# K and V loads of 8 MB in place of 4 MB, in an overlapping ring and a fixed buffer

## The chip, the cores and the metric

The kernel runs on one core of one Trainium2 chip. The metric is device time in microseconds (us), the median of several executions. Times of one kernel mostly repeat within about 0.1% here. The record calls a run slow when it is over 1.5% above the fastest of the same kernel.

## The reference, cut to what matters

One decoding step: attention of one query per head over a long cache of keys and values, times a small gated MLP.

```python
B, Sq, D = 2, 1, 512
Hq, Hkv, Sk, Dh = 32, 8, 32768, 128          # bf16 caches: B x Hkv x Sk x Dh
xn = layernorm(A_x)
q = (xn @ wq) ...                            # 4 query heads share one K/V head
p = softmax(q @ k^T * Dh ** -0.5)
s = (p @ v) ... @ wo
g = silu(mlp(xn))                            # w3, w4; w1 and w2 do not matter for one position
return A_x + s * g
```

K and V are 2 x 8 heads x 32768 x 128 x 2 bytes, 8 MB for each head and 268 MB in all. With the weights, 280.5 MB have to come from memory once, and each byte is used once. I call one (batch, K/V head) pair a head group; there are 16.

## The kernel before: the parts that matter

Each head group is cut into two halves of 16384 keys. A half of K, and a half of V, is one transfer of 4 MB: 128 partitions with 32 KB contiguous each. All large loads take the next of five equal slots.

```python
SLOT = KPT * Dh                              # 128 keys x 128: 32 KB per partition
slots = ctx.enter_context(tc.tile_pool(name="slots", bufs=5))

def load_cache(cache, b, g, i, name):
    t = slot(name)
    nc.sync.dma_start(
        out=t[:, :],
        in_=cache[b, g, i * NK:(i + 1) * NK, :].rearrange("(p t) d -> p (t d)", p=128),
    )
    return t
# ...
for n in range(NW + 1):                      # NW = 32 halves
    if n + 2 < NW:
        k_tiles[n + 2] = load_cache(A_k_cache, *work[n + 2], "k")
    if 0 < n + 1 < NW:
        v_tiles[n + 1] = load_cache(A_v_cache, *work[n + 1], "v")
    # ... at the last half: wo in three parts
    if n < NW:
        eps[n] = emit_k(n)                   # 8 transposes on DVE, 32 matmuls on PE, exp on ACT, pt on DVE
    if n == 1:
        emit_mlp()
    if n > 0:
        emit_v(n - 1, eps.pop(n - 1))        # 32 matmuls on PE
```

`emit_k` transposes a half of K on VectorE (eight operations into tile `T`) and multiplies it with the queries on TensorE. `emit_v` multiplies the exponentials `pt` with V.

The softmax here doesn't subtract the row's maximum and nothing guards it: scores larger than these inputs give would overflow.

Of the kernel before, what the change touches and what calls it, by code (L numbers as in the profile page):

```python
# [9 lines left out]
BF16 = mybir.dt.bfloat16  # L10
# [4 lines left out]
I32 = mybir.dt.int32  # L15

KPT = 128
RT = 16
VT = 4
SLOTS = 5  # L20
T_BUFS = 4
GELU_C = 0.7978845608028654
EPS = 1e-5
# [3 lines left out]
def kernel(  # L27
# [14 lines left out]
    nc = tc.nc  # L42

    B, Sq, D = A_x.shape
    _, Hkv, Sk, Dh = A_k_cache.shape
    HD = A_wq.shape[1]
    Hq = HD // Dh
# [2 lines left out]
    assert Sq == 1 and Dh == 128 and rep == 4 and D == 512 and Fdim % 128 == 0  # L50
    DK = D // 128
    FK = Fdim // 128
    NK = 128 * KPT
    assert Sk % NK == 0
    NPART = Sk // NK
    NR = KPT // RT
    NB = Dh // 64
    ZC = 128 + (NR - 1) * rep
# [2 lines left out]
    SLOT = KPT * Dh  # L61
# [2 lines left out]
    QP = 32 * (NQ - 1) + B  # L64

    pers = ctx.enter_context(tc.tile_pool(name="pers", bufs=1))
    slots = ctx.enter_context(tc.tile_pool(name="slots", bufs=SLOTS))
    ktp = ctx.enter_context(tc.tile_pool(name="ktp", bufs=T_BUFS))
    epp = ctx.enter_context(tc.tile_pool(name="epp", bufs=2))
    ptp = ctx.enter_context(tc.tile_pool(name="ptp", bufs=3))  # L70
# [4 lines left out]
    sc_ps = ctx.enter_context(tc.tile_pool(name="sc_ps", bufs=2, space=bass.MemoryType.PSUM))  # L75
    o_ps = ctx.enter_context(tc.tile_pool(name="o_ps", bufs=2, space=bass.MemoryType.PSUM))

    def slot(name):
        return slots.tile([128, SLOT], BF16, tag="slot", name=name)

    def load_cache(cache, b, g, i, name):
        t = slot(name)
        nc.sync.dma_start(
            out=t[:, :],
            in_=cache[b, g, i * NK:(i + 1) * NK, :].rearrange("(p t) d -> p (t d)", p=128),
        )
        return t


    x_bf = pers.tile([B, D], BF16)  # L90
    nc.scalar.dma_start(out=x_bf[:, :], in_=A_x[:, 0, :])
    wq_t = slot("wq")
    nc.sync.dma_start(  # L93
        out=wq_t[:, 0:DK * HD],
        in_=A_wq.rearrange("(p k) f -> p (k f)", k=DK),
# [3 lines left out]
    nc.gpsimd.memset(x4_bf[:, :], 0.0)  # L99
    for n in range(NQ):  # L100
        nc.gpsimd.dma_start(out=x4_bf[32 * n:32 * n + B, :], in_=A_x[:, 0, n * QW:(n + 1) * QW])
    work = [(b, g, i) for b in range(B) for g in range(Hkv) for i in range(NPART)]
    k_tiles, v_tiles = {}, {}
    k_tiles[0] = load_cache(A_k_cache, *work[0], "k0")
    k_tiles[1] = load_cache(A_k_cache, *work[1], "k1")
    w34 = slot("w34")
    W4O = DK * Fdim
    nc.sync.dma_start(out=w34[:, 0:W4O], in_=B_w3.rearrange("(p k) f -> p (k f)", k=DK))
    nc.sync.dma_start(out=w34[:, W4O:W4O + FK * D], in_=B_w4.rearrange("(p f) d -> p (f d)", f=FK))
    v_tiles[0] = load_cache(A_v_cache, *work[0], "v0")  # L110


    ident = pers.tile([128, 128], BF16)
# [6 lines left out]
    for j in range(4):  # L120
        nc.vector.tensor_copy(
            out=sel[:, :, :, j, :],
            in_=ident[:, :].rearrange("p (b w e) -> p b e w", b=NB, e=2),
# [4 lines left out]
        out=sel_o[:, :, :],  # L128
        in_=ident[:, :].rearrange("p (j a t h) -> p a t h j", j=4, t=VT, h=rep)[:, 0, :, :, :],
# [4 lines left out]
        out=sel_h[:, :],  # L134
        in_=ident[:, :].rearrange("p (r h) -> p h r", h=rep),
# [4 lines left out]
    for j in range(4):  # L140
        nc.vector.tensor_copy(
            out=sel_r[:, :, j, :],
            in_=ident[:, :].rearrange("p (w r) -> p r w", r=NQ),
# [3 lines left out]
    for r in range(NQ):  # L147
        nc.vector.tensor_reduce(
            out=mask[:, r, :],
            in_=ident[:, :].rearrange("p (h w) -> p h w", h=rep),  # L150
# [40 lines left out]
    for s, src in enumerate((xn_bf, ln2_bf)):  # L191
        for k in range(DK):
            c = (s * DK + k) * B
# [24 lines left out]
    for nb in range(NB):  # L218
# [9 lines left out]
        out=qr[:, :, :, :, :].rearrange("p n e b h -> p (n e b h)"),  # L228
# [54 lines left out]
            )  # L283
        return z

    def emit_k(n):
        b, g, i = work[n]
        if i == 0:
            state["z"] = emit_z(b, g)
        z = state["z"]  # L290
        kt = k_tiles.pop(n)[:, :].bitcast(I32)
        sc = sc_ps.tile([128, RT * 32], F32, tag="sc", name="sc")
        W = RT * NB * 32
        for r in range(NR):
            T = ktp.tile([128, W], I32, tag="T", name="T")
            nc.vector.transpose(  # L296
                out=T[:, :].rearrange("p (b t k) -> p t b k", b=NB, t=RT),
                in_=kt[:, r * W:(r + 1) * W].rearrange("p (t b k) -> p t b k", b=NB, t=RT),
            )
            Tb = T[:, :].bitcast(BF16).rearrange("p (b c e) -> p b c e", b=NB, e=2)  # L300
            zc = (NR - 1 - r) * rep
            for nb in range(NB):
                for e in range(2):
                    nc.tensor.matmul(  # L304
                        sc[:, :],
                        lhsT=z[:, nb, e, zc:zc + 128],
                        rhs=Tb[:, nb, :, e],
                        start=(r == 0 and nb == 0 and e == 0),
                        stop=(r == NR - 1 and nb == NB - 1 and e == 1),
                    )  # L310
        ep = epp.tile([128, RT * 32], BF16, tag="ep", name="ep")
        rs = smp.tile([128, 1], F32, tag="rs", name="rs")
        nc.scalar.activation(out=ep[:, :], in_=sc[:, :], func=ACT.Exp, scale=inv_sqrt_dh, accum_out=rs[:, :])  # L313
        pt = ptp.tile([128, NR, RT * rep], BF16, tag="pt", name="pt")
        nc.vector.transpose(  # L315
            out=pt[:, :, :].rearrange("p r (t h) -> p t r h", h=rep),
            in_=ep[:, :].rearrange("p (t r h) -> p t r h", r=NR, h=rep),
        )
        return pt, rs

    def emit_v(n, ep):
        b, g, i = work[n]
        pt, rs = ep
        vt = v_tiles.pop(n)[:, :].rearrange("p (t d) -> p t d", d=Dh)
        if i == 0:
            state["o"] = o_ps.tile([128, VT * Dh], F32, tag="o", name="o")
            nc.vector.memset(state["o"][:, :], 0.0)  # L327
            state["s"] = f_ps.tile([128, rep], F32, tag="f", name="S")
        o, S = state["o"], state["s"]
        sm = smp.tile([128, rep], F32, tag="sm", name="sm")  # L330
        nc.vector.tensor_scalar_mul(out=sm[:, :], in0=sel_h[:, :], scalar1=rs[:, 0:1])  # L331
        nc.tensor.matmul(S[:, :], lhsT=ones_f[:, :], rhs=sm[:, :], start=(i == 0), stop=(i == NPART - 1))  # L332
        for u in range(KPT // VT):
            r, a = divmod(u, RT // VT)
            j = u % 4
            nc.tensor.matmul(  # L336
                o[32 * j:32 * j + VT * rep, :],
                lhsT=pt[:, r, a * VT * rep:(a + 1) * VT * rep],
                rhs=vt[:, u * VT:(u + 1) * VT, :].rearrange("p t d -> p (t d)"),
                start=(i == 0 and u < 4), stop=(i == NPART - 1 and u >= KPT // VT - 4),  # L340
                tile_position=(0, 32 * j),
            )
        if i == NPART - 1:
            ob = obp.tile([128, VT * Dh], F32, tag="ob", name="ob")
            nc.scalar.copy(out=ob[:, :], in_=o[:, :])  # L345
            oT = f_ps.tile([128, rep], F32, tag="f", name="oT")
            for t in range(VT):
                nc.tensor.matmul(  # L348
                    oT[:, :], lhsT=ob[:, t * Dh:(t + 1) * Dh], rhs=sel_o[:, t, :],
                    start=(t == 0), stop=(t == VT - 1),  # L350
                )
            rec = smp.tile([128, rep], F32, tag="rec", name="rec")
            nc.vector.reciprocal(out=rec[:, :], in_=S[:, :])  # L353
            on = smp.tile([128, rep], BF16, tag="on", name="on")
            nc.vector.tensor_mul(out=on[:, :], in0=oT[:, :], in1=rec[:, :])  # L355
            xp = f_ps.tile([128, NQ, rep], F32, tag="f", name="xp")
            for r in range(NQ):
                nc.tensor.matmul(  # L358
                    xp[:, r, :], lhsT=sel_r[:, r, :, :].rearrange("p j w -> p (j w)"), rhs=on[:, :],
                    start=True, stop=True,  # L360
                )
            xm = smp.tile([128, NQ, rep], F32, tag="xm", name="xm")
            nc.vector.tensor_mul(out=xm[:, :, :], in0=xp[:, :, :], in1=mask[:, :, :])  # L363
            with nc.allow_low_precision(reason="three of the four terms are zero, the fourth is bf16"):
                nc.vector.tensor_reduce(out=oX[:, g, :, b], in_=xm[:, :, :], axis=AX.X, op=ALU.add)

    wo_parts = [(0, 4), (4, 7), (7, 8)]
    NW = len(work)
    eps = {}
    for n in range(NW + 1):  # L370
        if n + 2 < NW:
            k_tiles[n + 2] = load_cache(A_k_cache, *work[n + 2], "k")
        if 0 < n + 1 < NW:
            v_tiles[n + 1] = load_cache(A_v_cache, *work[n + 1], "v")
        if n == NW - 1:
            wo_t = slot("wo")
            wo3 = wo_t[:, 0:Hq * D].rearrange("p (g c) -> p g c", g=Hkv)
            wos = A_wo.rearrange("(g p r) d -> p g (r d)", p=128, r=NQ)
            for a, z in wo_parts:
                nc.sync.dma_start(out=wo3[:, a:z, :], in_=wos[:, a:z, :])  # L380
        if n < NW:
            eps[n] = emit_k(n)
        if n == 1:
            emit_mlp()
        if n > 0:
            emit_v(n - 1, eps.pop(n - 1))

    s_ps = pro_ps.tile([128, QW], F32, tag="pro")
    nc.vector.memset(s_ps[:, :], 0.0)
    for gr in range(Hkv * NQ):  # L390
        g, r = divmod(gr, NQ)
# [48 lines left out]
```

## Time and profile before

| | before |
|---|---|
| time, median of 3 | 661.64 us |
| span of the profiled run | 660.0 us |
| bytes read, rate over the span | 280.5 MB, 425 GB/s |
| load queue's share of the 16 DMA engines | 98.7% |
| PE, DVE busy | 63%, 53% |

These are lines of the page of the kernel before. The row of digits gives the busy share of the DMA engines in each of 40 slices of the span, in tenths (9 is 90% or more). The rows q1 and q8 give packets, MB and share of 16 engines' time; q1 is the load queue, q8 brings instructions.

```profile
span 660.0 us, 6356 instructions
...
PE 415.5 (63%) x2684; PEld 175.7 (27%) x2684; DVE 347.9 (53%) x442; ACT 50.1 (8%) x152; POOL 6.9 (1%) x20
...
DMA  9999999999999999999999999999999999999995
...
q1 hardware_dynamic: 10728, 280.50, 98.7%
q8 instruction: 21, 0.34, 0.2%
...
HBM read 280.50 MB, written 0.00 MB: 425 GB/s over the span
```

The DMA row is at 9 everywhere except in the last slice. No other engine comes near. From the table of waits (engine, line, what it waited for: us in total, times, longest) and the list of DMA issues (count, KB each, median us from issue to landing) of the same kernel:

```profile
DVE T L296 <- DMA k<-in_A_k_cache_dram: 167.7, 31, 7.1
...
k<-in_A_k_cache_dram SPq DMA_DIRECT2D x32, 4096.0 KB, 44.9
v<-in_A_v_cache_dram SPq DMA_DIRECT2D x32, 4096.0 KB, 39.2
```

The transposes wait for K in 31 of the 32 halves, all but the second. A K load is issued 44.9 us before it lands although 4 MB take only 9.7 us: four or five transfers stand in the queue at a time. The last lines to read are the end of the timeline of before (start, duration, engine, line, operation):

```profile
654.33 1.88 PE L394 MATMUL s_ps<-wo,oX 128*2 128x128 bf16 x64 [2.08 <-DMA wo<-in_A_wo_dram]
...
656.65 0.29 DVE L404 TENSOR_TENSOR out<-sg,x 98x128 bf16<-98x128 f32 x1
656.97 0.65 SPq L406 DMA_DIRECT2D out_dram<-out  x1
```

The output projection waits for wo, which is the last load. Its last packet ends at 655.18 us in the trace's packet records; what follows, about 5 us, is, with the 1.8 us ahead of the first packet, all of the kernel that no load covers.

### The profile page before, as it was taken

To read this page: it belongs to the slowest core of one execution; us is meant where nothing else is said; L and a number is where in the kernel's file an instruction comes from. 1 tells how busy PE (TensorE), PEld (TensorE's weight loads), DVE (VectorE), ACT (ScalarE), POOL (GpSimd) and SP (SyncE) were. 2 spreads that over 40 slices of the span, in tenths; PEclk is the share of its full clock that TensorE was granted. 3 is DMA by queue.
4 is the path that set the end of the run, shared out by engine and by line. 5 is a ranking of instruction groups with operands and counts; after the bars stand their busy time and mean duration, and the time that the engine had idled before them with its cause. 6 is when DMAs were issued, how large, how long until landed. Compare 5 with 4: busy or idle time off the path is not lost.

```text
span 660.0 us, 6356 instructions
## 1 busy us (share of the span) xinstructions
PE 415.5 (63%) x2684; PEld 175.7 (27%) x2684; DVE 347.9 (53%) x442; ACT 50.1 (8%) x152; POOL 6.9 (1%) x20
## 2 busy tenths in 40 slices
PE   2485667565566766467776566766646775656664
PEld 2242223222222322223222122322212232222222
DVE  5563456564445655445656444665644466554450
ACT  1111100000000000000000000000000000000000
POOL 3000000000000000000000000000000000000000
PEclk9985897676888767678777777877778787768886
DMA  9999999999999999999999999999999999999995
GB/s 382 419 437 442 418 438 439 424 439 425 434 436 427 439 428 429 440 427 434 437 425 437 432 429 440 425 434 439 427 435 428 435 436 427 437 434 429 432 419 232
DMA packets 11024, 280.91 MB, mean 426 GB/s; under 512 B 1386, under 2 KB 1396, under 8 KB 2420
## 3 DMA queue, kind: packets, MB, share of 16 engines
q1 hardware_dynamic: 10728, 280.50, 98.7%
q8 instruction: 21, 0.34, 0.2%
q0 software_dynamic: 256, 0.01, 0.0%
q14 instruction: 7, 0.06, 0.0%
q10 hardware_dynamic: 12, 0.00, 0.0%
HBM read 280.50 MB, written 0.00 MB: 425 GB/s over the span
## 4 chain that ended last, share of the span: by engine, by line
DMA 75%; PE 14%; DVE 7%; issue 2%; ACT 0%; SPq 0%; DVEq 0%; ACTq 0%
DMA k<-in_A_k_cache_dram 70%; PE sc L304 10%; DVE T L296 7%; DMA wo<-in_A_wo_dram 6%; PE o L336 3%; DVE pt L315 1%; ACT ep L313 0%; PE S L332 0%; PE s_ps L394 0%; DVE sm L331 0%; SPq L93 0%; SPq L380 0%; DVE sg L402 0%; DVE out L404 0%; DVEq L296 0%
## 5 line engine op out<-in xcount | busy, mean ns | idle before, releaser
L304 PE MATMUL sc<-T,z 128*128 128x512 bf16 x1024 | 301.1, 461 | 179.7 <-DVE T L296 179.5
L296 DVE STREAM_TRANSPOSE T<-k 128x1024 int32<-128x1024 int32 x256 | 292.1, 1207 | 167.7 <-DMA k<-in_A_k_cache_dram 167.7
L304 PEld LDWEIGHTS <-z 128*128 128x128 bf16 x1024 | 114.7, 112 | 365.1 <-issue 283.8
L336 PE MATMUL o<-v,pt 128*16 128x512 bf16 x1024 | 73.8, 439 | 4.9 <-DMA v<-in_A_v_cache_dram 4.9
L315 DVE STREAM_TRANSPOSE pt<-ep 128x512 bf16<-128x512 bf16 x32 | 22.8, 711 | 78.1 <-ACT ep L313 78.1
L313 ACT ACTIVATE ep<-sc 128x512 bf16<-128x512 f32 x32 | 19.1, 597 | 533.5 <-PE sc L304 533.5
L336 PEld LDWEIGHTS <-pt 128*16 128x16 bf16 x1024 | 25.4, 97 | 41.1 <-issue 23.7
L332 PE MATMUL S<-sm,ones_f 128*128 128x4 f32 x64 | 12.1, 260 | 24.8 <-DVE sm L331 24.8
L348 PE MATMUL oT<-sel_o,ob 128*128 128x4 f32 x128 | 16.9, 255 | 11.1 <-ACT ob L345 11.1
L348 PEld LDWEIGHTS oT<-sel_o,ob 128*128 128x128 f32 x128 | 15.5, 191 | 19.4 <-ACT ob L345 19.4
L332 PEld LDWEIGHTS S<-sm,ones_f 128*128 128x128 f32 x64 | 9.7, 191 | 32.5 <-DVE sm L331 32.5
L327 DVE MEMSET o<- 128x512 f32 x16 | 7.8, 485 | 13.4 <-ACT ob L345 12.3
L280 ACT COPY z<-qr 32x16 bf16<-32x16 bf16 x64 | 12.7, 198 | 11.6 <-DVE qr L227 10.9
L355 DVE TENSOR_TENSOR on<-oT,rec 128x4 bf16<-128x4 f32 x16 | 2.6, 161 | 20.2 <-PE oT L348 20.2
L345 ACT COPY ob<-o 128x512 f32<-128x512 f32 x16 | 9.4, 584 | 26.2 <-PE o L336 26.2
L353 DVE RECIPROCAL rec<-S 128x4 f32<-128x4 f32 x16 | 2.9, 182 | 7.3 <-PE S L332 7.2
L358 PEld LDWEIGHTS <-sel_r 128*128 128x128 bf16 x64 | 5.2, 117 | 5.2 <-issue 5.2
L209 PE MATMUL qT_ps<-xT,wq 128*128 128x2 bf16 x128 | 3.6, 165 | 4.5 <-DMA wq<-in_A_wq_dram 4.5
L358 PE MATMUL xp<-on,sel_r 128*128 128x4 bf16 x64 | 3.8, 164 | 4.0 <-DVE on L355 4.0
L313 ACT ACTIVATION_READ_ACCUMULATOR ep<-sc 128x1 f32 x32 | 6.3, 198 | 0.2
L331 DVE TENSOR_SCALAR sm<-sel_h,rs 128x4 f32<-128x4 f32 x32 | 6.0, 188 | 0.0
L363 DVE TENSOR_TENSOR xm<-xp,mask 128x16 f32<-128x16 f32 x16 | 2.8, 174 | 5.3 <-PE xp L358 5.3
(63 smaller groups left out, 48.5 us busy)
## 6 DMA issues: line engine op xcount, KB each, us to landing
k<-in_A_k_cache_dram SPq DMA_DIRECT2D x32, 4096.0 KB, 44.9
v<-in_A_v_cache_dram SPq DMA_DIRECT2D x32, 4096.0 KB, 39.2
wq<-in_A_wq_dram SPq DMA_DIRECT2D x1, 4096.0 KB, 12.5
w<-in_B_w_dram SPq DMA_DIRECT2D x2, 1792.0 KB, 38.0
wo<-in_A_wo_dram SPq DMA_DIRECT2D x1, 2048.0 KB, 34.4
wo<-in_A_wo_dram SPq DMA_DIRECT2D x1, 1536.0 KB, 37.8
wo<-in_A_wo_dram SPq DMA_DIRECT2D x1, 512.0 KB, 38.5
x_bf<-in_A_x_dram POOLq DMA_DIRECT2D x4, 0.5 KB, 9.6
```

The source lines that it names most:

```text
L280: nc.scalar.copy(out=z[32 * j:32 * j + 32, :, :, c:c + rep], in_=qr[32 * j:32 * j + 32, :, :, b, g * rep:(g + 1) * rep],)
L296: nc.vector.transpose(out=T[:, :].rearrange("p (b t k) -> p t b k", b=NB, t=RT), in_=kt[:, r * W:(r + 1) * W].rearrange("p (t b k) -> p t ...
L304: nc.tensor.matmul(sc[:, :], lhsT=z[:, nb, e, zc:zc + 128], rhs=Tb[:, nb, :, e], start=(r == 0 and nb == 0 and e == 0), stop=(r == NR - 1 ...
L313: nc.scalar.activation(out=ep[:, :], in_=sc[:, :], func=ACT.Exp, scale=inv_sqrt_dh, accum_out=rs[:, :])
L315: nc.vector.transpose(out=pt[:, :, :].rearrange("p r (t h) -> p t r h", h=rep), in_=ep[:, :].rearrange("p (t r h) -> p t r h", r=NR, h=rep),)
L327: nc.vector.memset(state["o"][:, :], 0.0)
L331: nc.vector.tensor_scalar_mul(out=sm[:, :], in0=sel_h[:, :], scalar1=rs[:, 0:1])
L332: nc.tensor.matmul(S[:, :], lhsT=ones_f[:, :], rhs=sm[:, :], start=(i == 0), stop=(i == NPART - 1))
L336: nc.tensor.matmul(o[32 * j:32 * j + VT * rep, :], lhsT=pt[:, r, a * VT * rep:(a + 1) * VT * rep], rhs=vt[:, u * VT:(u + 1) * VT, :].rearr ...
L345: nc.scalar.copy(out=ob[:, :], in_=o[:, :])
L348: nc.tensor.matmul(oT[:, :], lhsT=ob[:, t * Dh:(t + 1) * Dh], rhs=sel_o[:, t, :], start=(t == 0), stop=(t == VT - 1),)
L358: nc.tensor.matmul(xp[:, r, :], lhsT=sel_r[:, r, :, :].rearrange("p j w -> p (j w)"), rhs=on[:, :], start=True, stop=True,)
```

## The change

The intent is longer contiguous runs and fewer transfers. K and V of a head group become one transfer of 8 MB each, 64 KB contiguous per partition. Five slots of 32 KB are not enough for two double-buffered 64 KB tiles, so K lives in a ring of three 32 KB units: group m uses units 0 and 1 or units 1 and 2, and the next K may start once the shared unit 1 has been transposed, which is why that half is taken first. V has one fixed buffer of 64 KB, refilled when all V matmuls of a group are done. The MLP moves to the front, because its weights lie in V's buffer. The last group's loads stay in two halves.

```diff
-    slots = ctx.enter_context(tc.tile_pool(name="slots", bufs=SLOTS))
+    rings = ctx.enter_context(tc.tile_pool(name="rings", bufs=1))
...
+    kbuf = rings.tile([128, 3 * SLOT], BF16, name="kbuf")
+    vbuf = rings.tile([128, 2 * SLOT], BF16, name="vbuf")
+
+    def row_view(cache, b, g):
+        return cache[b, g, :, :].rearrange("(p t) d -> p (t d)", p=128)
+
+    def load_k(b, g, base, parts=1):
+        w = NPART * SLOT // parts
+        src = row_view(A_k_cache, b, g)
+        for c in range(parts):
+            nc.sync.dma_start(
+                out=kbuf[:, base * SLOT + c * w:base * SLOT + (c + 1) * w],
+                in_=src[:, c * w:(c + 1) * w],
+            )
+    # load_v(b, g, parts=1): the same into vbuf
...
-    for n in range(NW + 1):
-        ...
+    emit_mlp()
+    load_v(*groups[0])
+    for m in range(NG):
+        last = m == NG - 1
+        hs = (1, 0) if m % 2 == 0 else (0, 1)
+        eps = [emit_k(m, hs[0], True)]
+        if not last:
+            load_k(*groups[m + 1], (m + 1) % 2, 2 if m == NG - 2 else 1)
+        eps.append(emit_k(m, hs[1], False))
+        for i in range(NPART):
+            emit_v(m, hs[i], i, eps[i])
+        if not last:
+            load_v(*groups[m + 1], 2 if m == NG - 2 else 1)
+        if m == NG - 2:
+            # wo in three parts, into unit 0 of the K ring
```

More of the change, by code (lines that the diff above doesn't have):

```diff
@@ L19 @@
 VT = 4
-SLOTS = 5
 T_BUFS = 4
@@ L52 @@
     FK = Fdim // 128
-    NK = 128 * KPT
-    assert Sk % NK == 0
-    NPART = Sk // NK
+    NPART = 2
+    assert Sk == 128 * KPT * NPART
     NR = KPT // RT
@@ L76, with load_v @@
     o_ps = ctx.enter_context(tc.tile_pool(name="o_ps", bufs=2, space=bass.MemoryType.PSUM))
-    def slot(name):
-        return slots.tile([128, SLOT], BF16, tag="slot", name=name)
-    def load_cache(cache, b, g, i, name):
-        t = slot(name)
-        nc.sync.dma_start(
-            out=t[:, :],
-            in_=cache[b, g, i * NK:(i + 1) * NK, :].rearrange("(p t) d -> p (t d)", p=128),
-        )
-        return t
+    kbuf = rings.tile([128, 3 * SLOT], BF16, name="kbuf")
[10 more added lines that the diff above has]
+            )
+    def load_v(b, g, parts=1):
+        w = NPART * SLOT // parts
+        src = row_view(A_v_cache, b, g)
+        for c in range(parts):
+            nc.sync.dma_start(out=vbuf[:, c * w:(c + 1) * w], in_=src[:, c * w:(c + 1) * w])
     x_bf = pers.tile([B, D], BF16)
     nc.scalar.dma_start(out=x_bf[:, :], in_=A_x[:, 0, :])
-    wq_t = slot("wq")
+    wq_t = kbuf[:, 2 * SLOT:3 * SLOT]
     nc.sync.dma_start(
@@ L101 @@
         nc.gpsimd.dma_start(out=x4_bf[32 * n:32 * n + B, :], in_=A_x[:, 0, n * QW:(n + 1) * QW])
-    work = [(b, g, i) for b in range(B) for g in range(Hkv) for i in range(NPART)]
-    k_tiles, v_tiles = {}, {}
-    k_tiles[0] = load_cache(A_k_cache, *work[0], "k0")
-    k_tiles[1] = load_cache(A_k_cache, *work[1], "k1")
-    w34 = slot("w34")
+    groups = [(b, g) for b in range(B) for g in range(Hkv)]
+    NG = len(groups)
+    w34 = vbuf[:, 0:SLOT]
     W4O = DK * Fdim
@@ L109 @@
     nc.sync.dma_start(out=w34[:, W4O:W4O + FK * D], in_=B_w4.rearrange("(p f) d -> p (f d)", f=FK))
-    v_tiles[0] = load_cache(A_v_cache, *work[0], "v0")
+    load_k(*groups[0], 0)
     ident = pers.tile([128, 128], BF16)
@@ L284, in emit_z, with emit_k @@
         return z
-    def emit_k(n):
-        b, g, i = work[n]
-        if i == 0:
+    def emit_k(m, h, first):
+        b, g = groups[m]
+        if first:
             state["z"] = emit_z(b, g)
         z = state["z"]
-        kt = k_tiles.pop(n)[:, :].bitcast(I32)
+        u = m % 2 + h
+        kt = kbuf[:, u * SLOT:(u + 1) * SLOT].bitcast(I32)
         sc = sc_ps.tile([128, RT * 32], F32, tag="sc", name="sc")
@@ L319, in emit_k, with emit_v @@
         return pt, rs
-    def emit_v(n, ep):
-        b, g, i = work[n]
+    def emit_v(m, h, i, ep):
+        b, g = groups[m]
         pt, rs = ep
-        vt = v_tiles.pop(n)[:, :].rearrange("p (t d) -> p t d", d=Dh)
+        vt = vbuf[:, h * SLOT:(h + 1) * SLOT].rearrange("p (t d) -> p t d", d=Dh)
         if i == 0:
@@ L367 @@
     wo_parts = [(0, 4), (4, 7), (7, 8)]
-    NW = len(work)
-    eps = {}
-    for n in range(NW + 1):
-        if n + 2 < NW:
-            k_tiles[n + 2] = load_cache(A_k_cache, *work[n + 2], "k")
-        if 0 < n + 1 < NW:
-            v_tiles[n + 1] = load_cache(A_v_cache, *work[n + 1], "v")
-        if n == NW - 1:
-            wo_t = slot("wo")
-            wo3 = wo_t[:, 0:Hq * D].rearrange("p (g c) -> p g c", g=Hkv)
+    emit_mlp()
[12 more added lines that the diff above has]
+        if m == NG - 2:
+            wo3 = kbuf[:, 0:Hq * D].rearrange("p (g c) -> p g c", g=Hkv)
             wos = A_wo.rearrange("(g p r) d -> p g (r d)", p=128, r=NQ)
@@ L380 @@
                 nc.sync.dma_start(out=wo3[:, a:z, :], in_=wos[:, a:z, :])
-        if n < NW:
-            eps[n] = emit_k(n)
-        if n == 1:
-            emit_mlp()
-        if n > 0:
-            emit_v(n - 1, eps.pop(n - 1))
     s_ps = pro_ps.tile([128, QW], F32, tag="pro")
```

## The prediction

> **What bounds it now.** The DMA. The page's slice table shows the 16 DMA engines at 9 tenths in all but the last slice, the queue table gives the load queue 98.7% of their span, and 280.5 MB at 425 GB/s fill the 660.0 us span. Counted packet by packet in the trace, no engine idles between 1.8 us and about 650 us. PE is busy 63%, DVE 53%; in the table of waits the K transposes (L296) wait 167.7 us for K loads. Only the ends are not transfer: 1.8 us ahead of the first packet, about 5 us after wo's last packet (655.2 us). So two things can change the time: how fast the bytes move, and whether the new buffers let the queue run dry.
>
> **What the change does to the bytes.** Same bytes, larger packets. In the packet records a 32 KB packet takes 1213 ns nearly always, 14 KB 535 ns, 4 KB 159 ns: a line of about 0.0368 ns per byte plus 8 ns per packet. I estimate a 64 KB packet at 2419 ns against 2 x 1213 = 2426. K and V are 512 packets of 32 KB per engine; all but the last group's become half as many, so an engine saves about 240 x 8 ns = 1.9 us and about 30 completion packets of 9 ns, 0.3 us. Sum: 2.2 us, or 0.3%, all on the critical path. The Trainium skill ("DMA: Bandwidth & Descriptors", Where 436 GB/s comes from) puts the ceiling of the 16 ports at 435.2 GB/s; 32 KB packets run at 432 here, so under 1% is to be won.
>
> **What it moves.** Prefetch becomes shallower. The next K is issued when the first half of this K has been transposed (9.1 us in the timeline, 10 with PE), while this V transfers for 19.4 us: 9 us to spare. The next V is issued after all V matmuls: K's landing plus two halves of 9.5 us, exp and pt 2 us, V matmuls of 1.9 to 3.6 us twice, in sum 25 to 30 us, against 38.8 us until the queue has ended the next K: 9 us to spare. At the start V0 now waits for the MLP, whose weights arrive by about 21 us (before K0) and which needs about 9 us, while K0 transfers until about 41 us. At the end K and V (two halves each) and wo keep their order, so the tail of 5 us stays. The build's order of instructions shows waits by regions of the ring: no false wait ties the second half of K to the next load.
>
> **Predicted:** 659.4 us, 8 in 10 between 657.8 and 662.0. Faster by over 2%: 1%; within 2%: 95%; slower by over 2%: 4%.
>
> **What would show it.** The load queue has about 4000 packets fewer; 64 KB packets take about 2420 ns; DMA stays at 9 in every slice; the transposes' waits for K stay near 170 us in sum, in half as many, longer pieces; issue to landing of K about 29 us, of V 31 to 34 us.
>
> **What would make it wrong.** A 64 KB row might be cut into two descriptors: then about 661.6, no change. The engines' streams at 64 KB pitch could meet the memory less evenly and make packets longer than 2420 ns. A spare of 9 us could be eaten by an order on DVE or PE that I mis-read: each group would then show a hole in the DMA row. The small POOL loads may wait longer behind 64 KB packets and delay the MLP.

## The result, and the profile after

The changed kernel takes 660.80 us (median of 4, 660.72 to 661.1) against 661.76 us for the kernel before beside it. The ratio is 0.9989 with a 95% interval from 0.9974 to 1.0003. Ratios in this document are over fast runs; they are not quite the ratio of the medians that stand beside them (0.9985 here). In a second job of five rounds it took 660.80 us against 661.83 us, ratio 0.9985 (0.9973 to 0.9998). The first interval reaches just over 1, but in both jobs the slowest run of the changed kernel is faster than the fastest of the kernel before (661.10 against 661.49, 661.09 against 661.37 us). So the change is worth about 1 us, or 0.15%: real.

The same lines of the page after the change:

```profile
span 658.9 us, 6323 instructions
...
PE 386.7 (59%) x2652; PEld 172.1 (26%) x2684; DVE 346.0 (53%) x442; ACT 50.3 (8%) x152; POOL 6.9 (1%) x20
...
DMA  9999999999999999999999999999999999999995
...
q1 hardware_dynamic: 6408, 280.50, 98.6%
q8 instruction: 21, 0.34, 0.2%
...
HBM read 280.50 MB, written 0.00 MB: 426 GB/s over the span
```

The load queue has 4320 packets fewer, and the DMA row is as full as before. (PE's lower busy time is no effect to look for: 32 matmul records are missing from this trace, 2652 beside 2684 weight loads, and the clock granted to TensorE was higher in this execution, 0.825 of full speed against 0.787.) The waits and the issues of the changed kernel, the latter from the DMA view:

```profile
DVE T L303 <- DMA kbuf<-in_A_k_cache_dram: 150.5, 16, 15.0
...
kbuf<-in_A_k_cache_dram SPq DMA_DIRECT2D x15, 29.4
vbuf<-in_A_v_cache_dram SPq DMA_DIRECT2D x15, 31.7
```

The transposes wait about as long in sum, in half as many pieces. K is now issued 29.4 us before it lands, and 19.3 us of that is its own transfer: the stock in the queue is much smaller. The end of the timeline:

```profile
652.79 1.88 PE L400 MATMUL s_ps<-kbuf,oX 128*2 128x128 bf16 x64 [2.00 <-DMA kbuf<-in_A_wo_dram]
...
655.11 0.29 DVE L410 TENSOR_TENSOR out<-sg,x 98x128 bf16<-98x128 f32 x1
655.43 0.66 SPq L412 DMA_DIRECT2D out_dram<-out  x1
```

Everything at the end happens 1.54 us earlier and takes as long as before. The last packet of wo ends at 653.68 instead of 655.18 us. The span shrank by only 1.0 us because the store at the very end took about half a microsecond longer in this execution, which is of the size of the scatter between runs.

The packet records of the traces show the rest. Each transfer ends on each engine with a completion packet of 4 bytes. Recorded durations of packets that follow each other on one engine overlap by a few nanoseconds, so the cost of a packet is the distance from start to start, not the duration. Most common values, in ns, worked out from the packet records (8 KB from experiment e2; 32 KB and 64 KB from before and after):

```
packet   recorded duration   start to start   bytes at 27.2 GB/s   remainder
 8 KB          309               305.9              301.2             4.7
32 KB         1213              1209.4             1204.7             4.7
64 KB         2418              2414.1             2409.4             4.7
between two transfers: 6 ns more than inside one
```

The slope between 32 KB and 64 KB is 1204.7 ns for 32 KB, which is 27.2 GB/s per engine and 435.2 GB/s for 16. That is exactly the ceiling that the Trainium skill gives ("DMA: Bandwidth & Descriptors", Where 436 GB/s comes from). What a packet costs over its bytes is 4.7 ns, so at 32 KB the engines already ran at 99.6% of the ceiling. (The line is drawn through 32 and 64 KB; only 8 KB tests it. From the first completion packet of one 8 MB transfer to that of the next it is 19318.8 ns in after, 19356.4 in e1 and 19582.3 in e2, for 8, 16 and 64 packets: 4.7 ns per packet again, without sorting packets by engine.)

### The profile page after: what moved, and what is told of

Its sections match the earlier page's. It is cut to its first block, busy times and chain, and to the rows that moved or that the text cites. A ratio compares the mean times of both kernels' runs of the same rounds, so it can differ in the third digit from the quotient of the medians.

```text
span 658.9 us, 6323 instructions
## 1 busy us (share of the span) xinstructions
PE 386.7 (59%) x2652; PEld 172.1 (26%) x2684; DVE 346.0 (53%) x442; ACT 50.3 (8%) x152; POOL 6.9 (1%) x20
## 3 DMA queue, kind: packets, MB, share of 16 engines
q1 hardware_dynamic: 6408, 280.50, 98.6%
## 4 chain that ended last, share of the span: by engine, by line
DMA 75%; DVE 14%; issue 7%; PE 3%; SPq 0%; ACT 0%; DVEq 0%
DMA kbuf<-in_A_k_cache_dram 69%; DVE T L303 14%; DMA kbuf<-in_A_wo_dram 6%; PE sc L311 2%; PE o L343 1%; PE s_ps L400 0%; ACT ep L320 0%; SPq L95 0%; DVE pt L322 0%; SPq L115 0%; SPq L392 0%; SPq L114 0%; SPq L101 0%; PE S L339 0%; DVE sg L408 0%
## 5 line engine op out<-in xcount | busy, mean ns | idle before, releaser
L311 PE MATMUL sc<-T,z 128*128 128x512 bf16 x992 | 276.4, 421 | 206.3 <-DVE T L303 197.8
L303 DVE STREAM_TRANSPOSE T<-kbuf 128x1024 int32<-128x1024 int32 x256 | 291.5, 1205 | 150.5 <-DMA kbuf<-in_A_k_cache_dram 150.5
L311 PEld LDWEIGHTS <-z 128*128 128x128 bf16 x1024 | 105.7, 103 | 371.2 <-issue 278.7
L343 PE MATMUL o<-vbuf,pt 128*16 128x512 bf16 x1024 | 69.9, 434 | 3.2 <-DMA vbuf<-in_A_v_cache_dram 3.2
L343 PEld LDWEIGHTS <-pt 128*16 128x16 bf16 x1024 | 27.2, 99 | 37.9 <-issue 18.2
L339 PE MATMUL S<-sm,ones_f 128*128 128x4 f32 x64 | 10.7, 238 | 26.1 <-DVE sm L338 26.1
L355 PEld LDWEIGHTS oT<-sel_o,ob 128*128 128x128 f32 x128 | 15.5, 191 | 19.3 <-ACT ob L352 19.3
L215 PE MATMUL qT_ps<-xT,kbuf 128*128 128x2 bf16 x128 | 3.6, 165 | 4.5 <-DMA kbuf<-in_A_wq_dram 4.5
## 6 DMA issues: line engine op xcount, KB each, us to landing
kbuf<-in_A_k_cache_dram SPq DMA_DIRECT2D x15, 29.4
```

What stands on the lines that cost most here:

```text
L303: nc.vector.transpose(out=T[:, :].rearrange("p (b t k) -> p t b k", b=NB, t=RT), in_=kt[:, r * W:(r + 1) * W].rearrange("p (t b k) -> p t ...
L311: nc.tensor.matmul(sc[:, :], lhsT=z[:, nb, e, zc:zc + 128], rhs=Tb[:, nb, :, e], start=(r == 0 and nb == 0 and e == 0), stop=(r == NR - 1 ...
L339: nc.tensor.matmul(S[:, :], lhsT=ones_f[:, :], rhs=sm[:, :], start=(i == 0), stop=(i == NPART - 1))
L343: nc.tensor.matmul(o[32 * j:32 * j + VT * rep, :], lhsT=pt[:, r, a * VT * rep:(a + 1) * VT * rep], rhs=vt[:, u * VT:(u + 1) * VT, :].rearr ...
L355: nc.tensor.matmul(oT[:, :], lhsT=ob[:, t * Dh:(t + 1) * Dh], rhs=sel_o[:, t, :], start=(t == 0), stop=(t == VT - 1),)
```

## The experiments

Three questions were open. Is the gain of 1 us really the packets? Is the shallower queue as safe as I had said? And what sets the end, when engines finish at different times?

### e1 and e2: the same ring with smaller packets

The reading order of the keys within a group does not matter to softmax as long as K and V agree. So the new ring can be kept, transfer for transfer, while the source is cut in shorter runs. For e1:

```diff
     def row_view(cache, b, g):
-        return cache[b, g, :, :].rearrange("(p t) d -> p (t d)", p=128)
+        return cache[b, g, :, :].rearrange("(c p t) d -> p c (t d)", c=2, p=128)
```

with the same split of the destination. e2 has c=8, runs of 8 KB.

> The changed kernel with one edit: each 8 MB transfer reads the cache as (half, partition, 128 keys), so it is still one transfer into the same ring with the same waits, but a partition's row is two runs of 32 KB instead of one of 64 KB. Packets of 32 KB start 1209.4 ns apart in the trace of before and packets of 64 KB 2414.1 ns apart in the trace of after, so a 64 KB packet saves 4.7 ns per engine, 240 times. Theory (the gain is the packet overhead, by spacing): 1.1 us slower than the changed kernel, about 661.9 us. Rival A (the gain came from the ring and the new order of loads, packets don't matter): 660.8, as the changed kernel. Rival B (my prediction's 8 ns per packet, taken from durations): 1.9 us slower, 662.7. Packets of the load queue should rise by about 3840.

> As the one before, with eight runs of 8 KB per partition row: 2048 packets of K and V per engine instead of 272, 1776 more. Theory (4.7 ns per packet, by spacing): 8.3 us slower than the changed kernel, about 669.1 us. Rival B (8 ns per packet): 14.2 us slower, about 675.0. Rival A (packets don't matter): 660.8. Spacing of 8 KB packets: 306 ns (theory) or 309 (rival B).

Measured: e1 661.85 us (661.63 to 662.03; before 661.59), ratio 1.0004 (0.9991 to 1.0016). e2 669.10 us (669.04 to 669.23), ratio 1.0114 (1.0100 to 1.0128). The load queue of e1 and then of e2:

```profile
q1 hardware_dynamic: 10248, 280.50, 98.7%
```

```profile
q1 hardware_dynamic: 34824, 280.50, 99.4%
```

From e1 to e2 the share of busy DMA time rises although the rate falls, because the records count what a packet costs beyond its bytes as busy, and their overlaps twice: a busy share near 100% does not say how much of it moves bytes. Both times lie within 0.1 us of the sum with 4.7 ns per packet. Rival A is out: with 32 KB packets the ring and the new order of loads give back the whole gain. Rival B, my prediction's 8 ns, is out: it wanted 675.0 us for e2.

### e3: two transfers per load

```diff
-            load_k(*groups[m + 1], (m + 1) % 2, 2 if m == NG - 2 else 1)
+            load_k(*groups[m + 1], (m + 1) % 2, 2)
-            load_v(*groups[m + 1], 2 if m == NG - 2 else 1)
+            load_v(*groups[m + 1], 2)
```

(and the same for the first group).

> The changed kernel with every group's K and V in two transfers of 4 MB each (as its last group already is): 32 KB packets, and as many completions as before. In the traces the spacing across the end of a transfer is 6 ns more than inside one; 30 more ends are 0.2 us. Theory: packet cost 1.1 plus 0.2 us, about 662.1 us, the same as before within 0.5 us. Rival A (ring and order made the gain): below 661. Rival C (it is the number of transfers that cost, not of packets): clearly slower than the run with 32 KB runs in one transfer. Transposes may start half a transfer earlier; as the queue is always full that gives nothing.

Measured: 661.68 us (661.48 to 662.05; before 661.59), ratio 1.0002 (0.9989 to 1.0014). This is the kernel before's time with the changed kernel's schedule. It was meant to be 0.2 us slower than e1 for its extra completions and was 0.2 us faster, which is within the scatter, so the cost of a completion can't be seen in the times. Rival C is out: thirty more transfers of 4 MB cost nothing that can be measured.

### e4: the last group in whole transfers

```diff
-            load_k(*groups[m + 1], (m + 1) % 2, 2 if m == NG - 2 else 1)
+            load_k(*groups[m + 1], (m + 1) % 2)
-            load_v(*groups[m + 1], 2 if m == NG - 2 else 1)
+            load_v(*groups[m + 1])
```

> The changed kernel without the split of the last group's loads. By the timeline of after, the last K would land whole near 625 us instead of half at 615, its transposes end near 644 and the last exp and pt near 646.5; the last V lands at 644, then 64 V matmuls (3.6 to 6.8 us), 2.2 us to oX and 3 us of projection: end of the projection at 655 to 658.5 instead of 654.7. Theory (the tail is bound by the last wo packet only because the last loads are split): 0.5 to 4 us slower, 661.3 to 664.8. Rival (the split is without use, the queue's end rules): 660.7.

Measured: 660.88 us (660.69 to 661.83), ratio 0.9992 (0.9979 to 1.0006). I had expected it to be slower and it was not. The timeline of e4 at its end (lines between these are left out):

```profile
647.16 3.63 PE L343 MATMUL o<-vbuf,pt 128*16 128x512 bf16 x64
...
650.61 0.45 PE L400 MATMUL s_ps<-kbuf,oX 128*2 128x128 bf16 x18
...
652.96 1.56 PE L400 MATMUL s_ps<-kbuf,oX 128*2 128x128 bf16 x99
654.57 0.29 DVE L408 TENSOR_TENSOR sg<-s_ps,g 98x128 f32<-98x128 f32 x1 [1.12 <-PE s_ps L400]
```

The 64 V matmuls do start 3 us later than in the changed kernel (there the second half's start at 644.15), but all 64 together took 3.63 us, hardly longer than 32 took there (3.38). PE fills its waits with the parts of the projection that need only older groups, and `sg` starts at 654.57 instead of 654.71. So the split of the last group has no use in this kernel. It also makes e4 a second kernel with 64 KB packets in the same job as e1 to e3: 0.97 us less than e1.

### e5, e6 and e8: issuing the next K later

How far is the queue from running dry? A memset of two bytes into the shared ring unit, placed among the second half's transposes, makes the next K's load wait for that point. Nothing else changes, and there is no race, since the load overwrites what the memset wrote. For e5 (12 of 16 transposes done):

```diff
         for r in range(NR):
+            if r == at:                      # at = 4, second half
+                nc.vector.memset(kbuf[0:1, SLOT:SLOT + 2], 0.0)
             T = ktp.tile([128, W], I32, tag="T", name="T")
...
-        if not last:
-            load_k(*groups[m + 1], ...)
-        eps.append(emit_k(m, hs[1], False))
+        eps.append(emit_k(m, hs[1], False, None if last else 4))
+        if not last:
+            load_k(*groups[m + 1], ...)
```

e6 has the memset after all 16 transposes, e8 after 10.

> The changed kernel with the next K's issue tied to a point halfway through the second half's transposes: a two-byte memset into the ring unit that the next K overwrites stands after 12 of the 16 transposes, so the load has to wait for it. In the trace of after, K is issued about 9.2 us after its predecessor lands and the V in between transfers for 19.3 us, so about 9 us are to spare; this uses up about 5 of them. Theory (within its spare the time of issue is worth nothing): as the changed kernel, 660.8 within 0.5 us, DMA at 9 in all slices, K's issue to landing about 5 us shorter (about 24). Rival (shallower prefetch costs in proportion): clearly slower, by some 5 us or more.

> As the one before, with the memset after all 16 transposes of the group, 18.7 to 19.5 us after K's landing. V's transfer ends about 19.3 us after K's, landing is seen 0.5 us after the last packet and a first packet starts 1.0 us after its issue: so the spare is gone and a hole of 1 to 2 us opens in each of 15 groups. Besides, engines that ran ahead of the slowest now wait for it in every group instead of once at the end. Theory: 20 to 40 us slower, 681 to 701 us, with holes in the trace's packets at each K. Rival (the queue has slack elsewhere): 661 to 665.

Measured: e5 665.82 us (664.29 to 666.46; before 661.82), ratio 1.0057 (1.0045 to 1.0070). e6 704.73 us (703.23 to 707.61), ratio 1.0653 (1.0631 to 1.0675). Both miss: e5 should have cost nothing and cost 5.0 us, and e6 lies above the upper end of its range. One group of the changed kernel and then of e5, in the timeline, other lines between these left out; the SPq lines at L86 are the issues of K, that at L95 of V:

```profile
119.57 11.38 DVE L303 STREAM_TRANSPOSE T<-kbuf 128x1024 int32<-128x1024 int32 x10 [9.81 <-DMA kbuf<-in_A_k_cache_dram]
128.73 0.33 SPq L86 DMA_DIRECT2D kbuf<-in_A_k_cache_dram  x1
131.67 6.83 DVE L303 STREAM_TRANSPOSE T<-kbuf 128x1024 int32<-128x1024 int32 x6
146.93 0.33 SPq L95 DMA_DIRECT2D vbuf<-in_A_v_cache_dram  x1
```

```profile
120.17 11.38 DVE L305 STREAM_TRANSPOSE T<-kbuf 128x1024 int32<-128x1024 int32 x10 [11.04 <-DMA kbuf<-in_A_k_cache_dram]
132.51 3.50 DVE L305 STREAM_TRANSPOSE T<-kbuf 128x1024 int32<-128x1024 int32 x3
134.89 0.33 SPq L86 DMA_DIRECT2D kbuf<-in_A_k_cache_dram  x1
```

The issue moved from 9.2 us after the transposes' start to 14.7 us. The packet records tell why that was too much. This table has the time from K's issue to its first packet on any engine, over the 14 groups whose next K is one load, and the mean duration of the first 16 packets from there:

```
kernel             issue to first packet, us    first packets, ns
after                    6.0 to 8.0                2418 to 2480
e8 (10 of 16)            2.2 to 5.7                2418 to 2486
e5 (12 of 16)            1.0 to 2.9                2434 to 2946
e6 (16 of 16)            0.95 to 0.97              2944 to 3156
```

In e6 the queue is empty, so 0.96 us is what a first packet takes after its issue. (The Trainium skill, "DMA: Bandwidth & Descriptors", Latency and other measured facts, puts the first byte at about 0.6 us for this kind of queue; 0.96 us is measured here, from the issuing instruction's start.) In the changed kernel 5.1 to 7.0 us are therefore to spare, not the 9 us of my prediction. I had counted from landing to landing, which is the time of the slowest engine. The engines drift apart, by 3.0 to 4.5 us in the second half of the run (first to last completion packet of a transfer), and the fastest one is the first to ask for the next K. In e5 some engines stand still: an engine's mean idle time (the span less its load packets) rises by 1.3 us, and packets that restart after a gap are slow, together 4.4 us more per engine than in the changed kernel. In e6 it is 37 us of idle time and 10 us of slow packets. The sums, 5.7 and 46.9 us, are by this reckoning what the profiled executions lost (spans of 664.6 and 705.8 us against 658.9); the medians lost 5.0 and 43.9 us, because in both kernels the profiled execution was the slowest. The page of e6 shows the holes, where the changed kernel has a row of nines:

```profile
DMA  9998989989899998989989899997989999997996
...
q1 hardware_dynamic: 6408, 280.50, 93.4%
```

If this reading is right there is a threshold, and a smaller delay must be free. That was e8:

> As the run with K's issue halfway, but the memset stands after 10 of the 16 transposes, so K is issued about 2.5 us later than in the changed kernel. That run lost 5 us although I had counted 9 us to spare: in the trace of after, the first engine takes up the next K only 6.6 to 7.9 us after its issue ([...] landing is the slowest one's), and an empty queue needs 0.96 us from issue to first packet; so 5.6 to 6.9 us were to spare, and that run used 4.9 to 6.5. Theory (a threshold at the leading engine): here 3 to 4 us stay, no loss: 660.8 within 0.5, gap from issue to first packet of K 4 to 5.5 us, first packets at 2418 ns. Rival (loss in proportion to the delay): about half of that run's 5 us, 663.3.

(The 6.6 us of this text is the least of the first 11 groups; over all 14 it is 6.0 us, so the spare is smaller by as much.)

Measured: 660.87 us (660.73 to 660.99; the changed kernel beside it 660.80), ratio to before 0.9986 (0.9972 to 0.9999). No loss at all, with 2.2 to 5.7 us left to the first packet. In 13 of the 14 groups it is 2.8 us or more, and the first packets are no slower than in the changed kernel. In the last it is 2.2 us: there the first two packets take 2827 and 2554 ns, on the engines that lead, so the end does not move. The loss is not in proportion to the delay; it begins when the lead of an issue falls below about 3 us (at 2.8 us e8 shows no slow packet and e5 one of 2639 ns).

### e7: three quarters of V

Wrong result, to see whether time follows bytes when all compute stays.

```diff
     def load_v(b, g, parts=1):
-        w = NPART * SLOT // parts
+        w = NPART * SLOT * 3 // 4 // parts
...
+            uv = u - 16 if h == 1 and u >= 16 else u
-                rhs=vt[:, u * VT:(u + 1) * VT, :].rearrange("p t d -> p (t d)"),
+                rhs=vt[:, uv * VT:(uv + 1) * VT, :].rearrange("p t d -> p (t d)"),
```

> Wrong result on purpose: V's transfers bring 48 KB of each 64 KB row, and the last quarter of the V matmuls reads the third quarter again, so all compute stays and 33.55 MB fewer move. V then transfers for 14.5 us, still more than the 9.2 plus about 1.5 us to the next K's issue and start, so the queue should stay full. Theory (time is bytes at 27.2 GB/s per engine and nothing else): 256 packets of 48 KB for 64 KB per engine save 256 x 602.4 ns = 77.1 us for the bytes; with nothing lost in holes 583.7 us, 583 to 586. Rival (compute or the waits are near to binding too): well above 590.

Measured: 584.02 us (583.70 to 584.13), ratio 0.8825 (0.8811 to 0.8838). From the page of e7:

```profile
q1 hardware_dynamic: 6408, 246.94, 98.5%
...
HBM read 246.94 MB, written 0.00 MB: 424 GB/s over the span
```

33.55 MB fewer saved 76.8 us (660.80 less 584.02), against 77.1 us for those bytes at the engines' pace. Compute is not near to binding even with an eighth of the load gone, so a rearrangement of compute is no likely part of the change's effect. (The record marks e7's result as correct; its check did not notice the missing quarter of V.)

### e9 and e10: what holds the slowest engine

In the trace of after, the 16 engines end their last packets in three bunches: seven at 649.2 to 649.7 us, four at 652.0 to 652.2 and five at 653.5 to 653.7. The output waits for the last one. Instructions are fetched by the same engines. e9 repeats small matmuls that change nothing, so that there are more instructions to fetch:

```diff
-            for r in range(NQ):
+            for r in list(range(NQ)) * (17 if m < NG - 1 else 1):
                 nc.tensor.matmul(
                     xp[:, r, :], lhsT=sel_r[:, r, :, :].rearrange("p j w -> p (j w)"), rhs=on[:, :],
                     start=True, stop=True,
                 )
```

> The changed kernel with 960 harmless repeats of the four small matmuls of the exchange (start and stop each, same result), 16 per group and row, none in the last group. The page lists 21 instruction packets of 16 KB on the same 16 DMA engines; 1919 more instruction rows should make it about 28 or 29. PE has the time. In the trace of after the 16 engines end their wo packets in three bunches, 649.2 to 649.7, 652.0 to 652.1 and 653.4 to 653.7 us, which would fit no, two and three fetches of about 1.4 us each on an engine. Theory (the end is set by the engines that also fetch instructions): the last bunch 1.4 us later, about 662.2 us (661.5 to 663). Rival (fetches cost the load queue nothing, the bunches have another cause): 660.8 within 0.4.

> The changed kernel as it is, to stand beside the other two runs on the same chip: 660.8 within 0.3 us by both theories, ratio to before 0.9985 to 0.999.

Measured: e9 662.13 us (661.98 to 662.34), e10 660.80 us (660.73 to 661.09), before 661.83 us in the same job. The queues of e9:

```profile
q1 hardware_dynamic: 6408, 280.50, 98.4%
q8 instruction: 28, 0.46, 0.2%
```

Seven more packets of 16 KB, 0.1 MB of 281, cost 1.33 us, more than the whole change brought. Spread over all engines they would be about 0.4 us (7 x 0.93 us recorded duration / 16). In e9's trace the first bunch, again seven engines, still ends at 649.3 to 649.8 us while the last engines end at 654.6 to 654.75, 1.1 us later than in after. The completion packets show the step itself. In the second half of after's run the 16 engines keep their distances from one transfer to the next within about 2 ns, but where an instruction fetch falls, one engine drops back by 1.42 us: the fetch at 418.5 us moves one from 1.573 to 2.994 us behind the leader, that at 519.8 us one from 1.391 to 2.812. Seven engines, the first bunch, keep their places from 272 us to the end; the fetches fall on the other nine. So the end of this kernel is set by the engines that also fetch instructions. The records carry no engine number, so which engines these are stays open, and so do some smaller steps (0.3 to 0.85 us) that meet no fetch. The kernel before has 21 fetches too and ends in the same three bunches, so they are no part of the change's effect. That the repeats cost time on PE itself is not the cause: the last group has none of them, and PE has idle time in all others.

No run points to a version that is clearly better than the changed kernel. e4 and e8 equal it within 0.1 us.

## Why the prediction was right, and where it was off

- **The bound.** Right. DMA stays at 9 in 39 of 40 slices, and e7 shows time following bytes, 76.8 us measured for 77.1.
- **The size of the gain.** The mechanism was right and the size was double: 2.2 us predicted, 1.0 us measured (660.80 against 661.76 and 661.83). The step that failed is "about 0.0368 ns per byte plus 8 ns per packet". I took the 8 ns from recorded durations. Start to start a packet costs 4.7 ns over its bytes, and e2 measured that in the time itself. With it the sum is 240 x 4.7 ns = 1.1 us and 30 ends of transfers at 6 ns, 0.2 us: 1.3 us. The last packet in fact came 1.5 us earlier, and e1 against e4 gives 0.97 us for the packets alone.
- **A 64 KB row is one packet.** Right: 6408 packets instead of 10728, of 2418 ns where I had said about 2420. The pitch of 64 KB between rows did no harm.
- **The queue does not run dry.** Right in the result, but the number was wrong: "9 us to spare" for K is 5.1 to 7.0 us. The step that failed is counting from the slowest engine's landing to the slowest engine's end, with nothing for the 0.96 us that an issue needs to its first packet. e5 found it out by losing 5 us where I saw 4 us in hand.
- **Start and end.** Right. V0 was issued at 25.05 us, long before K0 landed at 42, and the small loads did not delay the MLP. The tail is as long as it was. The split of the last loads, which I had thought necessary for that, is not (e4).
- **Waits and landings.** Right: 150.5 us in 16 waits where about 170 in half as many were forecast; K 29.4 us and V 31.7 us from issue to landing, forecast 29 and 31 to 34.

## What to carry to other kernels

When the load engines are full from end to end and already run at 99.6% of their pace, larger transfers can only win back what a packet costs beyond its bytes; measure that from start to start of packets, not from their durations, and multiply by the number per engine. The rule for large transfers in the Trainium skill ("DMA: Bandwidth & Descriptors", Rules for kernel authors: 128 partitions and at least 1 MiB per DMA) was long fulfilled at 4 MB, and 8 MB brought 0.15%. Issuing later was free here as long as each load was issued some 3 us before the fastest engine needed it, and leads of 1.0 to 2.9 us cost 5 us, so check that lead in the trace, over all groups, before calling a ring safe.

## What the Trainium skill lacked or had wrong

- "Runtime: NRT & Kernel Launch", Instruction fetch mechanics: it calls the cost of crossing a 16 KiB block of instructions "mostly hidden". For the load queue of this kernel it is not: seven more such blocks (28 for 21) cost 1.33 us of 661 (e9). That fetches leave the engines unequal, so that some end 4.5 us ahead of others (649.2 to 653.7 us), is on no page that I read.
- "DMA: Bandwidth & Descriptors", Why small descriptors are slow: it speaks of a fixed overhead of about 3 cycles per packet, which at that page's 850 MHz is an estimate of 3.5 ns. The runs show 4.7 ns, four such cycles, on one line through packets of 8, 32 and 64 KB, and no further loss for runs of 64 KB.
- The same page's table of measured bandwidth ends at 425 GB/s for one 16 MB transfer. A queue that is never empty runs 32 KB packets at 433.5 GB/s here (16 x 32768 B / 1209.4 ns), 99.6% of the page's 435.2.
- The same page gives the time to a first byte, but not what restarting an engine costs: after a gap the first 16 packets of 64 KB took 2.9 to 3.2 us in the mean instead of 2.42 (e6), and 0.96 us from issue to first packet into an empty queue is what was seen there.
